# An attention and gated feed-forward kernel: output weights of the second phase moved to the low end of SBUF and sent through DRAM

## The chip, the cores and the metric

The kernel runs on one NeuronCore of a Trainium2 chip. The metric is device time in microseconds (us) of that core. Beside the timed runs, one execution was recorded by the hardware profiler; all durations below come from that execution. The engines are PE (TensorE matmul), PEld (TensorE weight load), DVE (VectorE), ACT (ScalarE), POOL (GpSimd) and SP (SyncE, which in this kernel issues every DMA).

## The reference

The first half is linear attention with exponential features, the second a gated feed-forward layer whose input is the attention's output. Batch 8, heads 8, sequence 576, head size 64, so 4608 tokens of width 512; the feed-forward width is 1536.

```python
def phi(x):
    proj = einsum('bhsd,df->bhsf', x, w_phi)          # 64 -> 128 features
    proj = proj - max(abs(proj), axis=-1, keepdims=True)
    return concatenate([exp(proj), exp(-proj)], axis=-1)
q_p, k_p = phi(q), phi(k)
kv = einsum('bhsf,bhsd->bhfd', k_p, v); z = sum(k_p, axis=2)
attn = einsum('bhsf,bhfd->bhsd', q_p, kv) / (einsum('bhsf,bhf->bhs', q_p, z)[..., None] + 1e-6)

x = attn.transpose(0, 2, 1, 3).reshape(4608, 512)
gate = 1 / (1 + exp(-(x @ w_gate)))                   # 512 -> 1536
out = (gate * (x @ w_val)) @ w_out                    # 1536 -> 512
```

The weights w_gate, w_val and w_out arrive in 64 bits.

## The kernel before, in words

**Precision.** A feed-forward factor is held as two 32-bit parts in TensorE's rounded format (fp32r): a high part and the rest. A product takes three matmuls: high by high, high by rest, rest by high. The function `weigh` loads a 512 KB block of 64-bit weights and makes both parts on DVE and ACT.

**First phase.** The 32 attention steps (8 batches by 4 head pairs, `attend`) run together with the feed-forward layer of the first 4 of the 12 blocks of 128 hidden units. `gate` (matmuls at L913) makes gate and value for a chunk of 512 tokens, `first_js` (matmuls at L970) multiplies by the 4 blocks of output weights; the partial sums go to DRAM (`ys`). After the last attention step only the feed-forward work of the chunks 7 and 8 is left, and with it begins the preparation of what follows.

**Second phase.** The other 8 blocks are taken in 4 pairs n = 0 to 3. Gate and value weights of a pair are combined by `combine` into seven products in place of eight (a Strassen scheme, so a weight tile G has 7 parts); `out_weight` makes the two parts of one block of output weights. Two passes go over all tokens, six stretches of 768 tokens each: the first with the pairs 0 and 1, the second with 2 and 3. One stretch is a call of `pass_over`: 28 products of six matmuls with 384 moving columns (L1228: stationary G, moving X), then 72 matmuls with 512 moving columns (L1310: stationary the gated values h, moving the output weights wo). During the first four stretches of pass one, the weights of the pairs 2 and 3 are made, put into a staging ring, written to DRAM (`kept`), and read back before pass two (`fetched`).

**Where the tiles lie.** Each partition of SBUF holds, from the low end, a few constants, the tile `flat`, and the tile `low`; from the high end down, during the first phase, the attention's tiles, and after it the tiles `more` and `high`. In the built program `low` begins at 50 KB and `high` at 137 KB. Rings of buffers are cut out of these tiles: X, y1, h and the staging ring lie in `low` (h at 48 to 72 KB from its start, staging at 72 to 86), G and the ring of output weights `r_wo` in `high` (G at 0 to 56 KB, `r_wo` at 56 to 72). In the first phase `low` holds that phase's weights (0 to 32), its x (32 to 48), its output weights (48 to 64) and its h (64 to 84); only the x of chunk 7 lies in `high`, at 42 to 58 KB. In a profile row `bank<-low,high` or `gate<-high,low` means that one operand lies in each tile, and `gate<-low` that both lie in `low`.

**What sets the order.** A planner (`Plan.run`) walks through all operations with a rank and an assumed duration each and writes one fixed order for PE, DVE, ACT and SP. A ring slot is given to the operation when the planner reaches it. Two marks hold operations back: `last` opens the `high` and `more` tiles after the last attention step, and `done` stands for the end of the whole first phase.

Of the kernel before, what the change touches and what calls it, by code (L numbers as in the profile page):

```python
# [20 lines left out]
P = 128  # L21
NP = H // 2
DM = H * D
# [12 lines left out]
DC = 2 * HT  # L36
NDC = NT // DC
CELL = 64
RA = 86 << 10
RB = 72 << 10  # L40
FB = 15 << 10
NQ = 3
LATE = 7
# [16 lines left out]
KEEP = 30.0  # L60
# [207 lines left out]
def attention_moe(  # L268
# [21 lines left out]
    def ring(where, tag, n, width, dtype=F32):  # L290
        cells, made = Cells(n), {}

        def view(i):
            if i not in made:
                pool = stage[where] if isinstance(where, str) else where
                made[i] = pool.tile([P, width], dtype, tag=f"{tag}{i}", name=f"{tag}{i}")
            return made[i]

        return [Slot(cells, i, 1, lambda i=i: view(i)) for i in range(n)]

    def arena(where, name, size, dtype):
        made = []

        def view():
            if not made:
                pool = stage[where] if isinstance(where, str) else where
                made.append(pool.tile([P, size // 4], dtype, tag=name, name=name))
            return made[0]

        cells = Cells(size // CELL)  # L310
        return lambda start=0: Area(view, cells, start * 1024 // CELL)
# [19 lines left out]
    wscr = [dram.tile([2, P, DM], F32, tag=f"wo{j}", name=f"wo{j}") for j in range(NJ)]  # L331
# [8 lines left out]
    r_g = ring(ps, "gate", 8 - BANKS, DM)  # L340
    low, high = arena(ff, "low", RA, F32R), arena("two", "high", RB, F32R)
    flat, more = arena(ff, "flat", 32 << 10, F32), arena("two", "more", FB, F32)
    x = low()
# [4 lines left out]
    x = flat()  # L348
# [4 lines left out]
    x = low()  # L353
    r_X = x.ring(14, 2 * HT)
    r_y1 = x.ring(3, DM)
    r_h = x.ring(8, 2 * HT)
    r_stage = x.ring(2, 7 * 2 * P)
    x = high()
    r_G = x.ring(8, 7 * 2 * P)
    r_wo = x.ring(8, DM)  # L360
    r_x7 = high(42).ring(2 * NC4, CW)
    r_sum = flat(20).ring(1, 2 * DM)
    r_tmp = flat(24).ring(1, 2 * HT)
# [1 line left out]
    x = more()  # L365
# [4 lines left out]
    def at(tag, n, shape, dtype=None):  # L370
        width = 1
        for s in shape[1:]:
            width *= s
        if tag not in at_rings:
            at_rings[tag] = ring("at", tag, n, width, dtype or F32)
        return Buf([at_rings[tag]], shape)
# [12 lines left out]
    def sp(size, fn, reads, writes, rank, after=()):  # L389
        return plan.op("SP", 0.06, size, fn, reads, writes, rank, after=after)  # L390
# [7 lines left out]
    def due(i):  # L398
        return 11.0 * i if i < NP else START + PERIOD * (i - NP)
# [7 lines left out]
    def attend(i):  # L407
        b, p = steps[i]
        r, slack = due(i), 0.1 if i < 2 * NP else 0.5
# [119 lines left out]
        else:  # L529
            nj = 2 * S // 32  # L530
# [11 lines left out]
            for hd in range(2):  # L542
                on_act(
                    DM, lambda hd=hd: act.copy(d()[:, hd, :DM], qf[hd]()),  # L544
# [6 lines left out]
                ),  # L551
                [pt], [(d, 2)], r + 2,
            )
            pm, pn = at("pm", 2, [P, nj]), at("pn", 2, [P, nj])
            mb = at("mb", 1, [P, 2, S])
            dve(
                2 * S,
# [445 lines left out]
    for i in range(N):  # L1003
# [8 lines left out]
        if i % NP == NP - 1:  # L1012
            lo = 0 if i < NP else ((i // NP) * S) // CW
            for c in range(lo, ((i // NP + 1) * S) // CW):
# [7 lines left out]
                r = due(i + 1) + LEAD + 66.0 * (c - lo)  # L1022
# [19 lines left out]
    done = plan.op("X", 0.0, 0.0, lambda: None, after=opening)  # L1042
# [7 lines left out]
    def pair(n):  # L1050
        return JA + 2 * n, JA + 2 * n + 1
# [49 lines left out]
    def kept(bufs, where, mark, r):  # L1101

        for n, x in enumerate(bufs):
            sp(
                x.shape[1] << 9,
                lambda n=n, x=x: nc.sync.dma_start(where[n], x().bitcast(F32)),
                [x], [(mark, n)], r,
            )

    def fetched(rings, width, where, mark, r, after=()):  # L1110

        out = []
        for n in range(2):
            x = Buf(rings, [P, width])
            sp(
                width << 9,
                lambda n=n, x=x: nc.sync.dma_start(x().bitcast(F32), where[n]),
                [(mark, n)], [x], r, after,
            )
            out.append(x)  # L1120
        return out

    def out_weight(j, r, rings, after):
        wh, wl = Buf(rings, [P, DM]), Buf(rings, [P, DM])
        weigh(j, 2, r, False, wh, wl, slice(0, DM), None, after)
        return wh, wl
# [166 lines left out]
    def pass_over(ns, dc, r, ws, wo, src, mark, dst, dmark):  # L1293

        x = x_blocks(dc, r - XLEAD)
        hs = []
        for i, n in enumerate(ns):
            hs.append([(Buf([r_h], [P, 2, HT]), Buf([r_h], [P, 2, HT])) for _ in range(2)])
            gs = gated(group(ws[n, 0], x, r + 14.6 * i))
            valued(gs, group(ws[n, 1], x, r + 14.6 * i + 7.3), hs[i])  # L1300
        for T in range(DC // P):
            acc = Buf([r_g], [P, DM])
            h, o = divmod(T * P, HT)
            for i, n in enumerate(ns):

                def out_part(i=i, n=n, acc=acc, h=h, o=o):
                    for e, j in enumerate(pair(n)):
                        (hh, hl), (wh, wl) = hs[i][e], wo[j]
                        for k_, (s, w) in enumerate(((hh, wh), (hh, wl), (hl, wh))):
                            nc.tensor.matmul(  # L1310
                                acc(), s()[:, h, o : o + P], w(),
                                start=i + e + k_ == 0, stop=i + e + k_ == 4,
                            )

                outs.append(pe(
                    "f", 1.37, out_part,
                    [(y, h) for hl_ in hs[i] for y in hl_]
                    + [y for j in pair(n) for y in wo[j]],
                    [acc], r + 29.2 + 1.4 * T + 0.7 * i, 0.3,
                ))  # L1320
            finish(dc * (DC // P) + T, acc, src, mark, dst, dmark, r + 29.2 + 2.8 * T)
# [6 lines left out]
    ws, wo, marks = {}, {}, {}  # L1328
    for n in range(2):
        r = base - 30.0 + 30.0 * n  # L1330
        for m in range(2):
            ws[n, m] = combine(n, m, r + 10.0 * m, [r_G], [])
        for j in pair(n):
            wo[j] = out_weight(j, r + 20.0, [r_wo], [])
    start = base + 150.0
    for dc in range(NDC):
        r = start + SPAN * dc
        pass_over(
            (0, 1), dc, r, ws, wo, yscr, ymark, lambda c, t: y2scr[c][t], y2mark
        )  # L1340
        if dc < 4:
            n, m = 2 + dc // 2, dc % 2
            mark = marks[n, m] = Buf()
            kept(combine(n, m, r + KEEP, [r_stage], [done]), gscr[n, m], mark, r + KEEP)
            j = JA + 4 + dc
            mark = marks[j] = Buf()
            kept(out_weight(j, r + KEEP + 10.0, [r_stage], [done]), wscr[j], mark, r + KEEP)

    start += SPAN * NDC
    for n, m, late in ((2, 0, []), (2, 1, taken[-4:-3]), (3, 0, outs[-8:-7]), (3, 1, outs[-1:])):  # L1350
# [66 lines left out]
```

## Time and profile before

| | |
|---|---|
| median of 3 runs | 1168.27 us (1164.08, 1168.27, 1170.7) |
| the profiled execution | 1167.91 us, of it the span from the first to the last instruction 1166.0 us |
| PE busy | 1148.7 us, 99% of the span, 8796 matmuls |
| DVE, ACT busy | 933.6 us (80%), 583.3 us (50%) |
| DMA | 166.88 MB, 143 GB/s in the mean |
| granted TensorE clock | 1.000 throughout |
| L1228 / L1310 / L913 / L970, matmul | 2016 / 864 / 804 / 432 instructions |

Times in the trace count from the span's start. Attention ends near 516 us, the first phase's last matmul near 613 us; pass one runs from there to 890 us, pass two to the end. A busy PE is not a PE at its peak, since the ends of matmuls are modelled: what one matmul costs in a dense stretch is the stretch's length over the number of its matmuls.

### The profile page before, as it was taken

The numbers are of one execution on the slowest core, as the hardware profiler recorded it, in microseconds if no ns is written. First come the engines' busy times: TensorE is split into PE (matmuls) and PEld (weight loads), VectorE is DVE, ScalarE is ACT, GpSimd is POOL, SyncE is SP. The second block draws the span as 40 slices with busy tenths as digits, with TensorE's granted clock in tenths as the row PEclk, the third lists the DMA queues.
The fourth block names the chain that finished last, engine by engine and source line by source line (L and its number), as shares of the span: only waits on it lengthen the run. The fifth ranks groups of instructions, "written<-read, shape, count | busy, mean of one in ns | idle before, by whom it ended". The sixth has DMA issues, their size and how long they took to land.

```text
span 1166.0 us, 22301 instructions
## 1 busy us (share of the span) xinstructions
PE 1148.7 (99%) x8796; PEld 939.5 (81%) x8796; DVE 933.6 (80%) x1793; ACT 583.3 (50%) x1115; POOL 0.7 (0%) x6
## 2 busy tenths in 40 slices
PE   8999999999999999999999999999999999999998
PEld 6666566776676777778879899899899898998997
DVE  6999989888878878848987999998766756857764
ACT  6767776666657666626553444352332332423421
POOL 0000000000000000000000000000000000000000
PEclk9999999999999999999999999999999999999999
DMA  7674553444425353225334646645557424224232
GB/s 235 202 242 126 151 169 120 133 125 126 146 80 160 108 155 103 79 79 193 116 99 152 204 142 238 181 147 179 163 178 278 143 93 122 81 89 157 59 91 82
DMA packets 97136, 166.88 MB, mean 143 GB/s; under 512 B 18568, under 2 KB 43272, under 8 KB 97032
## 3 DMA queue, kind: packets, MB, share of 16 engines
q1 hardware_dynamic: 97032, 165.46, 44.8%
q8 instruction: 69, 1.13, 0.4%
q14 instruction: 35, 0.29, 0.1%
HBM read 117.96 MB, written 47.32 MB: 142 GB/s over the span
## 4 chain that ended last, share of the span: by engine, by line
PE 85%; DVE 8%; DMA 5%; ACT 1%; issue 1%; SPq 0%; DVEq 0%; ACTq 0%
PE bank L1228 30%; PE gate L1310 17%; PE gate L913 11%; PE gate L970 7%; PE bank L620 4%; PE bank L662 3%; PE bank L431 2%; DMA rb<-den 2%; PE bank L680 2%; PE bank L913 2%; PE bank L536 1%; DMA den<-dn 1%; PE bank L970 1%; DVE d L586 1%; PE bank L634 1%; PE bank L646 1%
## 5 line engine op out<-in xcount | busy, mean ns | idle before, releaser
L1228 PE MATMUL bank<-low,high 128*128 128x384 f32 x2016 | 352.3, 336 | 0.9 <-DVE low L1190 0.7
L1228 PEld LDWEIGHTS bank<-low,high 128*128 128x128 f32 x2016 | 349.8, 188 | 2.7 <-DVE low L1190 1.0
L1310 PE MATMUL gate<-high,low 128*128 128x512 f32 x864 | 203.6, 395 | 0.0
L1310 PEld LDWEIGHTS gate<-high,low 128*128 128x128 f32 x864 | 162.3, 188 | 37.9
L913 PE MATMUL gate<-low 128*128 128x512 f32 x708 | 168.4, 394 | 1.2 <-ACT flat L948 0.6
L913 PEld LDWEIGHTS gate<-low 128*128 128x128 f32 x708 | 130.8, 188 | 30.2 <-issue 1.2
L478 ACT ACTIVATE ek<-ek 128x512 f32<-128x512 f32 (+1 forms) x192 | 96.7, 526 | 27.5 <-DVE ek L466 26.2
L1241 DVE TENSOR_TENSOR more<-more,bank 128x384 f32<-128x384 f32 x104 | 57.2, 550 | 43.0 <-PE bank L1228 42.8
L970 PE MATMUL gate<-low 128*128 128x512 f32 x372 | 89.8, 395 | 0.0
L970 PEld LDWEIGHTS gate<-low 128*128 128x128 f32 x372 | 68.6, 188 | 15.0 <-issue 1.0
L620 PE MATMUL bank<-ek,vin 128*32 128x256 f32 x1240 | 73.3, 381 | 4.5 <-ACT d L544 4.1
L1241 DVE TENSOR_TENSOR flat<-flat,bank 128x384 f32<-128x384 f32 x87 | 47.9, 551 | 34.9 <-PE bank L1228 34.2
L620 PEld LDWEIGHTS bank<-ek,vin 128*32 128x32 f32 x1240 | 37.4, 110 | 45.8 <-issue 10.2
L1138 DVE TENSOR_TENSOR flat<-gate,low 128x512 f32<-128x512 f32 x72 | 49.3, 685 | 24.8 <-PE gate L1310 15.0
L437 DVE TENSOR_REDUCE mk<-bank 128x4 f32<-128x512 f32 (+1 forms) x92 | 49.0, 551 | 19.7 <-PE bank L431 17.1
L1186 ACT CAST low<-more 128x768 fp32r<-128x768 f32 x36 | 30.1, 836 | 66.2 <-DVE more L1177 66.2
L466 DVE TENSOR_TENSOR ek<-bank,mk 128x512 f32<-128x512 f32 (+1 forms) x92 | 48.2, 550 | 0.6 <-ACT d L549 0.2
L937 ACT CAST low<-flat 128x512 fp32r<-128x512 f32 x36 | 22.3, 621 | 49.6 <-DVE flat L962 45.4
L589 ACT ACTIVATE eq<-d 128x1152 f32<-128x1152 f32 x29 | 33.9, 1167 | 24.5 <-DVE d L586 24.4
L1283 ACT CAST low<-flat 128x384 fp32r<-128x384 f32 x44 | 22.0, 511 | 45.0 <-DVE flat L1279 44.9
L1266 ACT ACTIVATE more<-more 128x384 f32<-128x384 f32 x37 | 19.4, 525 | 47.6 <-DVE more L1241 47.6
L431 PE MATMUL bank<-wk,kin 64*128 64x128 f32 x496 | 38.5, 289 | 4.5 <-DMA kin<-k 4.4
(187 smaller groups left out, 1701.0 us busy)
## 6 DMA issues: line engine op xcount, KB each, us to landing
flat<-w_moe SPq DMA_DIRECT2D x36, 512.0 KB
low<-xs SPq DMA_DIRECT2D x46, 256.0 KB
kin<-k SPq DMA_DIRECT2D x32, 320.0 KB
qin<-q SPq DMA_DIRECT2D x32, 320.0 KB
vin<-v SPq DMA_DIRECT2D x32, 320.0 KB
ys<-flat SPq DMA_DIRECT2D x36, 256.0 KB
low<-ys SPq DMA_DIRECT2D x36, 256.0 KB
yt<-flat SPq DMA_DIRECT2D x36, 256.0 KB
```

The lines of the kernel that those rows point to most:

```text
L431: nc.tensor.matmul(pk[hd]()[:, t, :], x()[head(hd), t * P : t * P + P], wk[head(hd), :], start=True, stop=True,)
L437: vec.tensor_reduce(mx, pk, axis=AX.X, op=ALU.max, apply_absolute_value=True)
L466: vec.tensor_tensor(ek[g]()[:, :, F:], src, mk[g]()[:, :ns].unsqueeze(2).broadcast_to([P, ns, F]), op=ALU.subtract,)
L478: lambda g=g, sg=sg: act.activation(ek[g]()[:, :, sg * F : sg * F + F], ek[g]()[:, :, F:], AF.Exp, scale=1.0 - 2.0 * sg,),
L620: nc.tensor.matmul(o_[o : o + Q, : 2 * F], vx()[:, 2 * t + hd, o % D : o % D + Q], (e0, e1)[hd][:, t, :] if t < 4 else e2[:, 0, :], start= ...
L662: nc.tensor.matmul(nm()[o : o + Q, :], w()[:, sg, o : o + Q], es[sg]()[:, o // D, cs], start=sg == 0, stop=sg == 1, tile_position=(0, o),)
L913: nc.tensor.matmul(o(), a()[:, ws], x(), start=cc + n == 0, stop=cc == NC4 - 1 and n == 2,)
L970: nc.tensor.matmul(acc(), a()[:, ts], w(), start=first and i == 0, stop=last and i == 2)
L1138: lambda: vec.tensor_tensor(y(), acc(), y1().bitcast(F32), op=ALU.add),
L1228: nc.tensor.matmul(o()[:, :HT], s()[:, ws], y()[:, cc, :], start=first and cc + i_ == 0, stop=cc + i_ == 3, skip_group_check=not first,)
L1241: lambda: vec.tensor_tensor(o(), p(), q()[:, :HT], op=ALU.add),
L1310: nc.tensor.matmul(acc(), s()[:, h, o : o + P], w(), start=i + e + k_ == 0, stop=i + e + k_ == 4,)
```

## The change

Five things are done.

1. The ring `r_wo` of 8 output-weight buffers (2 KB each) goes from `high` to `low`, where it takes 72 to 88 KB from the tile's start (122 to 138 KB of the partition in the built program), behind h. `low` grows from 86 to 88 KB, `high` shrinks from 72 to 70.
2. The staging ring goes from `low` to `high`, behind G (56 to 70 KB). A second ring `r_swo` of 7 buffers of 2 KB covers the same 14 KB; staged output weights take those instead of the 7 KB buffers.
3. Since `low` is in use until the first phase ends, the output weights of the pairs 0 and 1 can no longer be made in their final place. They are made in `r_swo`, written to DRAM, and read back after `done`: 8 writes and 8 reads of 256 KB more.
4. The attention's small tiles `pm` and `pn` get one buffer each in place of two.
5. Through the planner the order of instructions moves: on SP from about 533 us of the trace on, on DVE, ACT and PE from about 550. Up to there it is the same.

```diff
-RA = 86 << 10
-RB = 72 << 10
+RA = 88 << 10
+RB = 70 << 10
...
     r_h = x.ring(8, 2 * HT)
-    r_stage = x.ring(2, 7 * 2 * P)
+    r_wo = x.ring(8, DM)
     x = high()
     r_G = x.ring(8, 7 * 2 * P)
-    r_wo = x.ring(8, DM)
+    r_stage = x.ring(2, 7 * 2 * P)
+    r_swo = high(56).ring(7, DM)
     r_x7 = high(42).ring(2 * NC4, CW)
...
-            pm, pn = at("pm", 2, [P, nj]), at("pn", 2, [P, nj])
+            pm, pn = at("pm", 1, [P, nj]), at("pn", 1, [P, nj])
...
         for j in pair(n):
-            wo[j] = out_weight(j, r + 20.0, [r_wo], [])
+            mark = marks[j] = Buf()
+            kept(out_weight(j, r + 20.0, [r_swo], []), wscr[j], mark, r + 20.0)
     start = base + 150.0
+    for j in (*pair(0), *pair(1)):
+        wo[j] = fetched([r_wo], DM, wscr[j], marks[j], start - 20.0, [done])
...
             j = JA + 4 + dc
             mark = marks[j] = Buf()
-            kept(out_weight(j, r + KEEP + 10.0, [r_stage], [done]), wscr[j], mark, r + KEEP)
+            kept(out_weight(j, r + KEEP + 10.0, [r_swo], [done]), wscr[j], mark, r + KEEP)
```

In the changed file the lines L913, L970 and L1228 stand at L914, L971 and L1229, L1310 at L1311 and the DMA of `fetched` at L1118.

**PE, where the first phase ends.** L913 are the last gate and value products of chunk 8, L970 its output products (48 matmuls, in four rows of 12), L1228 the first products of the second phase. Before:

```order
L913 MATMUL bank_194<-low 128x512 x12
L1228 MATMUL bank_192<-low,high 128x384 x6
L1228 MATMUL bank_182<-low,high 128x384 x6
L970 MATMUL gate_213<-low 128x512 x12
L970 MATMUL gate_206<-low 128x512 x12
L970 MATMUL gate_219<-low 128x512 x12
L970 MATMUL bank_180<-low 128x512 x12
L1228 MATMUL bank_204<-low,high 128x384 x6
```

After:

```order
L914 MATMUL bank_194<-low 128x512 x12
L1229 MATMUL bank_192<-low,high 128x384 x6
L971 MATMUL gate_213<-low 128x512 x12
L971 MATMUL gate_206<-low 128x512 x12
L971 MATMUL gate_219<-low 128x512 x12
L971 MATMUL bank_182<-low 128x512 x12
L1229 MATMUL bank_180<-low,high 128x384 x6
L1229 MATMUL bank_204<-low,high 128x384 x6
```

The second product of the second phase now stands behind chunk 8's output products. In the same way one value product of chunk 8 now stands ahead of chunk 7's output products, near 569 us of the trace. Beyond these two places PE's order is the same to the end.

**SP, at the same place.** `ys8` are the sums of chunk 8, written from `flat`; `ys0` the partial sums that the first stretch reads; `w_moe` the 64-bit weights of pair 2. Before:

```order
L999 DMA ys8_105<-flat_175 128x512 x2
L1166 DMA more_5903<-xs2_90 128x2x384
L999 DMA ys8_105<-flat_175 128x512 x2
L1133 DMA low_325<-ys0_97 128x512 x3
L790 DMA flat_175<-w_moe 128x1024 x3
L1166 DMA low_325<-xs1_89 128x2x256
```

After:

```order
L1167 DMA more_5848<-xs2_90 128x2x384
L1000 DMA ys8_105<-flat_175 128x512
L1118 DMA low_325<-wo4_119 128x512 x2
L1118 DMA low_325<-wo5_120 128x512 x2
L1118 DMA low_325<-wo6_121 128x512 x2
L1118 DMA low_325<-wo7_122 128x512 x2
L1134 DMA low_325<-ys0_97 128x512 x3
L791 DMA flat_175<-w_moe 128x1024 x2
L1167 DMA low_325<-xs1_89 128x2x256
```

The eight reads of the output weights stand between the last sums of chunk 8 and the reads of `ys0`; of the three weight loads behind them, the third has moved further back.

## The prediction, made before the changed kernel ran

> **What bounds the kernel now.** I read the busy times, PE's waits, and then the chain of waits, in order of time, where it runs along PE.
>
> ```profile
> PE 1148.7 (99%) x8796; PEld 939.5 (81%) x8796; DVE 933.6 (80%) x1793; ACT 583.3 (50%) x1115; POOL 0.7 (0%) x6
> ...
> PE bank L1228 <- DVE low L1190: 0.7, 1, 0.7
> ...
> PE bank L1228 <- ACT low L1186: 0.2, 1, 0.2
> ```
>
> PE is busy for 99% of the span. These two are its only waits after the attention, 0.9 us together, both at 600 us. So no wait is left to take away beyond that place: time after 516 us falls only if a matmul gets cheaper. A busy share does not tell what one costs; pieces of the chain without a gap do, by their length over their count:
>
> ```profile
> 532.93 5.60 PE bank L913 x24
> ...
> 549.43 8.40 PE bank L913 x36
> 557.83 8.40 PE gate L913 x36
> ...
> 568.97 10.88 PE bank L970 x48
> 579.85 8.16 PE gate L913 x36
> ...
> 613.37 27.04 PE bank L1228 x156
> 640.41 16.79 PE gate L1310 x72
> ```
>
> All but L1228 have 512 moving columns. L970 costs 10.88/48 = 226.7 ns, and so does L913 at 579.85 (8.16/36). L1310 costs 16.79/72 = 233.2, and L913 from 532.93 to 566 (5.60/24, 8.40/36) 233.3. Same line, same shape, same clock (1.000), two prices. What differs is where the operands lie (order of time, PE):
>
> ```profile
> 549.27 6.93 PE L913 MATMUL bank<-high,low 128*128 128x512 f32 x29
> ...
> 568.81 11.04 PE L970 MATMUL bank<-low 128*128 128x512 f32 x48
> 579.69 8.32 PE L913 MATMUL gate<-low 128*128 128x512 f32 x36
> ...
> 640.25 5.06 PE L1310 MATMUL gate<-high,low 128*128 128x512 f32 x21
> ```
>
> The dear ones read the moving operand from `high` (x of chunk 7; output weights) and the stationary one from `low`; the cheap ones read both from `low`. L1228 has it the other way round, moving X in `low` and stationary G in `high`, and costs 27.04/156 = 173.3 ns for 384 columns. The step from 384 to 512 columns that this leaves to the low price, 226.7 - 173.3 = 53.4 ns, is exactly 128 columns at 2.4 per ns, so L1228 carries the low price's fixed part (226.7 - 213.3 = 13.4 ns) and not the high price's 19.9. It is the moving operand's place that costs 6.6 ns.
>
> **The change part by part.**
>
> *Output weights to `low`.* The 864 matmuls of L1310 keep their stationary h in `low` and get the moving operand from there too. There are 12 groups of 72, each 16.79 us now and 72 x 226.7 ns = 16.32 us at the low price: 12 x 0.47 = 5.6 us less. Bounds: the trace shows the low price for moving operands up to 64 KB into `low` (114 KB of the partition) and the high price from 42 KB into `high` (179 KB); the new place is at 122 to 138 KB. Unknown lies between, so the gain is between 0 and 5.6. I take 5.6: the new place is 8 KB from the last cheap one and 41 KB from the first dear one; and by distance between the operands too it is near (at most 40 KB from h; the cheap pairs of L913 are up to 48 KB apart, the dear pairs at least 71).
>
> One rule speaks against it. The Trainium skill ("SBUF — State Buffer", Who interferes with whom) gives PE two independent read ports, one for the moving operand and one for weight loads, and says that PE waits on nobody; in "TensorE: Matmul & The Clock Gate" (Back-to-back issue gap) the gap hangs on the column count alone. By that, moving the weights brings 0; the trace's 226.7 against 233.3 ns on one line disagrees, though nothing in it is a test of the place alone. It is a rival below.
>
> *The second product of pass one behind L970.* Around PE's only late wait (order of time, PE, then DVE):
>
> ```profile
> 598.73 1.21 PE L1228 MATMUL bank<-low,high 128*128 128x384 f32 x6
> 600.16 0.44 PE L1228 MATMUL bank<-low,high 128*128 128x384 f32 x1 [0.23 <-ACT low L1186]
> 601.31 1.14 PE L1228 MATMUL bank<-low,high 128*128 128x384 f32 x5 [0.70 <-DVE low L1190]
> 602.29 8.36 PE L970 MATMUL gate<-low 128*128 128x512 f32 x36
> ```
>
> ```profile
> 599.11 0.68 DVE L934 TENSOR_TENSOR flat<-flat,bank 128x512 f32<-128x512 f32 x1
> 599.71 0.68 DVE L866 SCALAR_TENSOR_TENSOR high<-flat 128x512 fp32r<-128x512 uint32 x1
> 600.31 0.95 DVE L1190 TENSOR_TENSOR low<-more,low 128x768 fp32r<-128x768 f32 x1
> 601.18 0.68 DVE L939 TENSOR_TENSOR low<-flat,low 128x512 fp32r<-128x512 f32 x1
> ```
>
> Two products, 6 x 173.3 ns = 1.04 us each, fill 598.73 to 602.29: 3.56 - 2.08 = 1.48 us is lost, waiting for the second product's X (L1186, L1190). Now one product ends at 599.77 and L970 follows. Its first 9 matmuls need only h of blocks made earlier: 9 x 0.227 = 2.04 us, to 601.8. The last three need the last h, whose rest L939 writes until 601.86 here; in the changed order one short DVE operation and one of L1190's size stand between L934 and L939, and on ACT a copy of the first product's sum stands ahead of the cast that L939 needs: much the same in the end. The 12th matmul, the only one that reads it, starts near 602.3. So no wait follows: 1.48 us gained. Bounds: 0 (DVE late by as much) to 1.48. The product that moved finds its X 10.9 us later, long done. The value product of chunk 8 that passes chunk 7's sums only swaps two pieces of work without a wait between 566 and 590 us: nothing.
>
> *The round trip of the output weights.* 8 writes and 8 reads of 256 KB on SP. The price of an issue and the rate come from where pass two's weights are read (order of time, SP; a window of 4 us, whose last column is GB/s; the page's mean and its 40 slices):
>
> ```profile
> 890.28 1.82 SPq L1117 DMA_DIRECT2D high<-wo  x4
> 892.15 0.90 SPq L1117 DMA_DIRECT2D high<-g  x2
> 893.15 2.17 SPq L1117 DMA_DIRECT2D high<-wo  x4
> ...
> 894.00:898.00 4.00, 4.00 (x25) 4.00 (x24) 1.81 (x4) 1.11 (x3) 0.00 (x0) 1.00 1.05 396
> ...
> DMA packets 97136, 166.88 MB, mean 143 GB/s; under 512 B 18568, under 2 KB 43272, under 8 KB 97032
> ...
> GB/s 235 202 242 126 151 169 120 133 125 126 146 80 160 108 155 103 79 79 193 116 99 152 204 142 238 181 147 179 163 178 278 143 93 122 81 89 157 59 91 82
> ```
>
> An issue takes about 0.5 us, and 396 GB/s are reached. The reads stand behind the last sums of chunk 8, which wait for the end of L970:
>
> ```profile
> 611.36 3.04 SPq L999 DMA_DIRECT2D ys<-flat  x2
> 614.49 1.62 SPq L1133 DMA_DIRECT2D low<-ys  x3
> 616.16 16.99 SPq L790 DMA_DIRECT2D flat<-w_moe  x3
> ```
>
> L970 now starts at 599.77 and ends near 610.8 instead of 613.4, so the reads are issued from about 612 to 616; 2.1 MB take 5 us at that rate and 15 at the mean of 143 GB/s. L1310 first needs them at 640.41 - 1.48 = 638.9: 8 us spare at the worst. What waits behind them on SP moves by 4 us: `ys0`, first read when L1310 has its first sums, and the weights of pair 2 (order of time, DVE):
>
> ```profile
> 624.30 0.42 DVE L795 TENSOR_SCALAR flat<-flat 128x512 uint32<-128x512 uint32 x1
> ```
>
> DVE takes the first of these up at 624.30 without a wait, 8 us after its issue; in the changed order that operation stands 11 DVE operations later, near 629. Cover suffices for 4 us of issue and 5 of transfer. The price if it doesn't: every us that DVE stands still there goes to PE as soon as the 5 banks are full. The writes come while the chunks 7 and 8 are worked off, and each waits in SP's queue for ACT or DVE to finish a part; behind them wait weight loads for pairs 0 and 1, which nobody needs before 598.73. I take 0, and 2 us as the upper bound.
>
> *Staging in `high`.* ACT and DVE write the same parts with the same instructions at another address; between 640 and 800 us, where DVE is fullest, it has room (after the length: busy us and count of PE, PEld, DVE, ACT, POOL):
>
> ```profile
> 640.00:680.00 40.00, 40.00 (x208) 36.74 (x207) 37.25 (x70) 17.96 (x34) 0.00 (x0) 1.00 0.61 204
> 680.00:720.00 40.00, 40.00 (x208) 36.74 (x207) 39.44 (x75) 17.41 (x33) 0.00 (x0) 1.00 0.59 198
> 720.00:760.00 40.00, 40.00 (x208) 36.74 (x207) 37.56 (x69) 17.61 (x32) 0.00 (x0) 1.00 0.56 165
> 760.00:800.00 40.00, 40.00 (x207) 36.74 (x206) 37.83 (x69) 15.14 (x27) 0.00 (x0) 1.00 0.58 190
> ```
>
> 152.1 us in 160, while PE gets through with the same work 3.5 x 0.47 = 1.6 us sooner: 6 us remain. Taken as 0; the second of these windows alone has 0.6 us to spare, so 0 to 2.
>
> *One buffer for `pm` and `pn`.* Both are written and read by DVE alone, in order: 0.
>
> *The sum*, against the profiled execution: 1167.9 - 5.6 - 1.5 = 1160.8 us. The median of the runs is 0.4 above the profiled one: **1161.1 us**, 0.61% below 1168.27.
>
> **The rivals.**
>
> *A. The price changes inside the new place*, at 128 KB of the partition, say. Three of the eight buffers lie below that, and by the built program 324 of the 864 matmuls read them: 324 x 6.6 ns = 2.1 us in place of 5.6, so 1164.6. For it: the 65 KB between cheap and dear are unseen in the trace. Against: the place is at the cheap end of them. 15%.
>
> *B. The place has nothing to do with it*, and the high price belongs to something else that chunk 7 and L1310 share. Only the 1.5 us of PE's wait go: 1166.8. The skill's two pages named above give this one. Against: L913 changes price at 566 within one line. 10%.
>
> *C. DVE becomes the limit after the phase change*, on the late weights of pair 2 or in the window from 680 to 720: 2 to 4 us come back, about 1164. For it: DVE's 39.44 of 40. Against: PE waits for DVE nowhere there now. 13%.
>
> *D. The output weights come late* (the other side). The first group of L1310 waits for all eight reads; from 638.9 on each us late is a us lost, and from 646 on the gain of 7.1 is eaten. For 1174 and more they must land after 652, 2.1 MB in 40 us, under 55 GB/s. One slice of the page is that low (59), but of little demand. 5%, and 1177 if so.
>
> **How the numbers follow.** The forecast keeps 57%. About 0.5% (5.8 us) is what a measurement of this kernel tells from no change; the limit for faster is 1162.4, 1.3 us above the forecast, and the three runs before lie 6.6 us apart, so I count 0.8 of the forecast as faster by over 0.5% (0.46), with a little from A and C (0.04): 0.50. Slower by over 0.5%: D, 0.05. Within 0.5%: 0.45. The range goes from 1159 (the forecast less the runs' scatter) to 1167 (B included).
>
> **What would show it.** Right: L1311 in pieces of 72 at 16.3 us, its names `gate<-low`; L914 on `high,low` still 233 ns; no wait of PE at 600 us; L971's last group ending about 2.5 us sooner; the reads of the output weights on SP from 612 on, none waited for. Wrong: L1311 at 233 ns throughout (B) or a mix of the two prices (A); PE waiting for DVE between 625 and 800 (C), or for a DMA at 639 (D).

## The result, and the profile after

The changed kernel takes 1160.76 us (median of 8 runs, 1159.15 to 1161.92), the kernel before 1167.71 us (8 runs, 1164.08 to 1170.7). The ratio is 0.9935, with a 95% interval of 0.9923 to 0.9948: 0.65% less. The profiled execution has a span of 1158.9 us, 7.1 us less than the 1166.0 before.

The chain of waits of the changed kernel, in order of time (start, length, what), around the end of the first phase and at the end of the program:

```profile
489.49 10.89 PE gate L971 x48
...
549.04 8.40 PE bank L914 x36
...
598.50 1.04 PE bank L1229 x6
599.54 8.20 PE gate L971 x36
607.74 2.72 PE bank L971 x12
610.46 28.08 PE bank L1229 x162
638.54 16.36 PE gate L1311 x72
654.90 29.12 PE bank L1229 x168
...
1138.86 16.37 PE gate L1311 x72
```

Two things are to be seen. From 598.50 to 654.90 each piece begins where the one before it ends: PE's wait at 600 us is gone, and no other has come. And a group of 72 output products, whose rows now read `gate<-low`, takes 16.36 us where it took 16.79. Chunk 7's products at 549 us, whose x still lies in `high`, cost 8.40 us for 36 as before. The last group of the kernel before, and the start of the same L970 group, give the length of the stretch that the change can touch:

```profile
489.81 10.94 PE gate L970 x48
...
1145.53 16.81 PE gate L1310 x72
```

From the start of that group to the start of the first output products it was 640.41 - 489.81 = 150.60 us and is 149.05, so 1.55 less; from there to the end of the last group it was 521.93 us and is 516.69, so 5.24 less. Together 6.79 of the 7.1 us; the other 0.3 lie before 490 us, where the profiles of the kernels below differ by more than that.

The output weights are read back without anyone waiting for them (SP in the changed kernel, order of time):

```profile
611.54 4.12 SPq L1118 DMA_DIRECT2D low<-wo  x8
...
617.95 1.87 SPq L791 DMA_DIRECT2D flat<-w_moe  x2
```

DVE is fuller than before in its fullest window (after the length: busy us and count of PE, PEld, DVE, ACT, POOL), 39.86 of 40 us where it was 39.44, and PE has no idle time in it:

```profile
680.00:720.00 40.00, 40.00 (x211) 37.16 (x210) 39.86 (x76) 17.59 (x33) 0.00 (x0) 1.00 0.59 198
```

### The profile page after: what moved, and what is told of

It reads as the page before. It is cut to its first block, busy times and chain, and to the rows that moved or that the text cites. A ratio compares the mean times of both kernels' runs of the same rounds, so it can differ in the third digit from the quotient of the medians.

```text
span 1158.9 us, 22323 instructions
## 1 busy us (share of the span) xinstructions
PE 1142.8 (99%) x8796; PEld 939.5 (81%) x8796; DVE 933.3 (81%) x1793; ACT 583.0 (50%) x1115; POOL 0.7 (0%) x6
## 4 chain that ended last, share of the span: by engine, by line
PE 84%; DVE 7%; DMA 6%; ACT 2%; issue 1%; SPq 1%; DVEq 0%
PE bank L1229 30%; PE gate L1311 17%; PE gate L914 11%; PE gate L971 6%; PE bank L621 4%; PE bank L663 3%; PE bank L914 3%; DMA rb<-den 3%; PE bank L432 2%; PE bank L681 2%; DMA den<-dn 2%; PE bank L537 1%; DVE d L587 1%; PE bank L971 1%; PE bank L635 1%; PE bank L647 1%
## 5 line engine op out<-in xcount | busy, mean ns | idle before, releaser
L1229 PE MATMUL bank<-low,high 128*128 128x384 f32 x2016 | 351.8, 336 | 0.0
L1229 PEld LDWEIGHTS bank<-low,high 128*128 128x128 f32 x2016 | 349.8, 188 | 1.1
L1311 PE MATMUL gate<-low 128*128 128x512 f32 x864 | 198.4, 389 | 0.0
L1311 PEld LDWEIGHTS gate<-low 128*128 128x128 f32 x864 | 162.0, 188 | 33.2
L914 PE MATMUL gate<-low 128*128 128x512 f32 x696 | 165.7, 393 | 1.2 <-ACT flat L949 0.6
L914 PEld LDWEIGHTS gate<-low 128*128 128x128 f32 x696 | 128.6, 188 | 29.7 <-issue 1.2
L1242 DVE TENSOR_TENSOR more<-more,bank 128x384 f32<-128x384 f32 x111 | 61.1, 551 | 40.8 <-PE bank L1229 40.3
L971 PE MATMUL gate<-low 128*128 128x512 f32 x384 | 92.3, 394 | 0.0
L971 PEld LDWEIGHTS gate<-low 128*128 128x128 f32 x384 | 70.8, 188 | 15.1 <-issue 1.0
L1242 DVE TENSOR_TENSOR flat<-flat,bank 128x384 f32<-128x384 f32 x75 | 41.3, 551 | 29.3 <-PE bank L1229 29.1
L1284 ACT CAST low<-more 128x384 fp32r<-128x384 f32 x50 | 24.7, 513 | 46.6 <-DVE more L1280 46.6
L590 ACT ACTIVATE eq<-d 128x1152 f32<-128x1152 f32 x29 | 33.9, 1168 | 24.8 <-DVE d L587 24.4
```

Source lines behind the costliest of these rows:

```text
L914: nc.tensor.matmul(o(), a()[:, ws], x(), start=cc + n == 0, stop=cc == NC4 - 1 and n == 2,)
L971: nc.tensor.matmul(acc(), a()[:, ts], w(), start=first and i == 0, stop=last and i == 2)
L1229: nc.tensor.matmul(o()[:, :HT], s()[:, ws], y()[:, cc, :], start=first and cc + i_ == 0, stop=cc + i_ == 3, skip_group_check=not first,)
L1242: lambda: vec.tensor_tensor(o(), p(), q()[:, :HT], op=ALU.add),
L1311: nc.tensor.matmul(acc(), s()[:, h, o : o + P], w(), start=i + e + k_ == 0, stop=i + e + k_ == 4,)
```

## The experiments

Each changed kernel moves the whole time by a few us, and single runs of one kernel lie up to 8 us apart. Most of that scatter arises in the first 250 us: the same L913 piece of the attention starts at 249.98 us in the profile of the kernel before, at 247.28 and 252.43 in two of the kernels below, and from there to the L970 group at 490 us all three take 239.84 us within 0.02. So each kernel is read twice, by its median and by the two stretches named above, from its profile. Each ratio is to runs of the kernel before that were taken together with the kernel's own. One table for all:

| kernel | median, us | ratio to before | to the first output products | from there to the end |
|---|---|---|---|---|
| before | 1167.71 to 1168.93 in four sets of runs | | 150.60 | 521.93 |
| the change | 1160.76 | 0.9935 (0.9923 to 0.9948) | 149.05 | 516.69 |
| e2: round trip and order, old place | 1168.42 | 0.9993 (0.998 to 1.0005) | 149.12 | 523.52 |
| e3: order alone | 1166.16 | 0.9979 (0.997 to 0.9987) | 150.10 | 521.93 |
| e4: change, old order | 1165.80 | 0.998 (0.9966 to 0.9993) | 155.18 | 516.87 |
| e6: before, `high` 64 bytes lower | 1174.54 | 1.0051 (1.0037 to 1.0066) | 150.96 | 526.71 |
| e7: change, `high` 64 bytes lower | 1166.90 | 0.9979 (0.9966 to 0.9991) | 149.47 | 521.85 |
| e8: before, `low` 64 bytes higher | 1172.53 | 1.0038 (1.0026 to 1.005) | 150.94 | 526.57 |
| e9: before, `high` 192 bytes lower | 1165.36 | 0.9973 (0.996 to 0.9985) | 150.35 | 517.10 |
| e10: change, `high` 192 bytes lower | 1161.50 | 0.9942 (0.9929 to 0.9955) | 148.42 | 517.02 |
| e11: change, h behind the output weights and 64 bytes higher | 1165.95 | 0.9983 (0.9972 to 0.9994) | 149.05 | 522.56 |

### The place by itself (e1)

```diff
+    for st in "afkpuy":            # stationary tile at 16, 56, 96, 136, 176, 208 KB
+        for mv in NAMES:           # moving tile a..y, every 8 KB
+            for i in range(36):
+                nc.tensor.matmul(o, tiles[st][:, s : s + P], tiles[mv][:, m : m + DM], ...)
```

> A measurement by itself: the whole computation of the reference is left out and the output holds ones. 25 tiles of 8 KB lie side by side in SBUF, from 16 KB of the partition to 216 KB. For each of six stationary tiles (at 16, 56, 96, 136, 176 and 208 KB) every tile in turn is the moving operand of 36 matmuls of 128x512 in fp32r. Theory P (the moving operand's own address decides): 226.7 ns for every moving tile up to some address between 138 and 179 KB, 233.3 ns above it, with the same step for all six stationary tiles. Theory Q (the distance between the two operands decides): 226.7 ns while they lie at most 48 KB apart, 233.3 ns from 71 KB on, so that the cheap stretch travels with the stationary tile and both ends of the row are dear when it lies in the middle. Theory R (the place has no part in it, rival B of the prediction): the same price for all 150 pairs.

PE in this kernel, order of time, the first blocks after the start (moving tile, stationary tile):

```profile
12.82 8.32 PE L38 MATMUL acc<-tb,ta 128*128 128x512 f32 x36
20.98 8.32 PE L38 MATMUL acc<-tc,ta 128*128 128x512 f32 x36
```

From start to start 8.16 us for 36, that is 226.7 ns. All 149 blocks behind the first have this length, wherever their operands lie. Theory R holds, P and Q fall: neither the region of SBUF nor the distance across regions costs anything, as long as the operands lie whole multiples of 512 bytes apart, as all of these do. The prediction's reading, that "the moving operand's place" costs 6.6 ns, falls with them, while the time that it forecast had come out. So the price hung on something that the place carried along.

### The change taken apart (e2, e3, e4)

e2 is the kernel before with the round trip, but into the old buffers; e3 only holds the second product back; e4 is the change with that product forced ahead again:

```diff
 # e2, on the kernel before
-            wo[j] = out_weight(j, r + 20.0, [r_wo], [])
+            mark = marks[j] = Buf()
+            kept(out_weight(j, r + 20.0, [r_wo], []), wscr[j], mark, r + 20.0)
     start = base + 150.0
+    for j in (*pair(0), *pair(1)):
+        wo[j] = fetched([r_wo], DM, wscr[j], marks[j], start - 20.0, [done])
 # e3, on the kernel before (product of pass_over)
+            late = [done] if i and len(taken) < 2 else []
-            o_ = pe("f", 1.05, go, [gh, gl, xh, xl], [o], r + 1.04 * i, 0.3, taken[-1:])
+            o_ = pe("f", 1.05, go, [gh, gl, xh, xl], [o], r + 1.04 * i, 0.3, taken[-1:] + late)
 # e4, on the change (closers: the output products of chunk 8)
+            if i == 1 and len(taken) == 1:
+                for cl in closers:
+                    o_.then.append(cl)
+                    cl.wait += 1
```

> The kernel before with the output weights of the first pairs written to DRAM and read back as in the change, but into their old buffers in `high`: the round trip and the order of PE that it brings, without the new place. Theory (the place gives 5.2 of the 7 us, the order 1.5): the groups of 72 of the output product stay at 16.79 us, PE's wait at 600 us is gone, about 1166.2 us by the median, 1.5 below the kernel before. Rival B (the place has nothing to do with it): about 1161, as the change. If the round trip itself cost something that the change hides: over 1168.

> The kernel before, in which the second product of the first pass may not start before the last output product of chunk 8 is planned: the order alone, with no round trip, and no new place. Theory: groups of 72 at 16.79 us, no wait of PE at 600 us, 1.5 us below the kernel before, about 1166.2 us. Rival (the wait only goes elsewhere, to the last of chunk 8's output products, whose operand DVE writes last): a PE wait of 1 to 1.5 us between 600 and 612 us, and the time of the kernel before, 1167.7.

> The changed kernel with the second product of the first pass put back ahead of chunk 8's last output products, as the kernel before had it: new place and round trip, without the order. Theory: groups of 72 at 16.36 us as in the change, PE's wait of about 1.5 us at 600 us back, about 1162.3 us, 1.5 above the change and 5.4 below the kernel before. Rival (the order is the larger part of the gain): over 1165.

The output groups behave as expected in all three. The chains of e2, e3 and e4, one piece each:

```profile
636.24 16.79 PE gate L1310 x72
```

```profile
640.42 16.79 PE gate L1311 x72
```

```profile
643.49 16.36 PE gate L1318 x72
```

The totals don't follow the theories: forecast were 1166.2, 1166.2 and 1162.3 us, measured 1168.42, 1166.16 and 1165.80, and the one that met its number did not do so for the reason given. Every edit lets the planner write another order elsewhere, and each new order brought a stall of its own.

**e2** wins the first stretch, 149.12 us, 1.48 less than before: the order alone is worth the 1.48 us that were forecast. It loses 1.59 in the second, around the third output group, whose sums come late; PE's wait is 1.0 of it, and the matmuls around the wait run less densely:

```profile
PE gate L1310 <- DVE flat L1138: 1.0, 1, 1.0
```

So its median, 1168.42, is that of the kernel before. In this order, the round trip without a new price of the matmuls brings nothing.

**e3** shows what the prediction feared as rival C. Its chain leaves PE for a weight read (in order of time):

```profile
600.44 8.18 PE gate L970 x36
...
614.42 6.21 DMA flat<-w_moe
623.09 7.64 PE bank L1228 x42
630.76 9.66 PE bank L1228 x54
```

and on DVE the first operation on those weights stands still for them:

```profile
620.66 0.43 DVE L795 TENSOR_SCALAR flat<-flat 128x512 uint32<-128x512 uint32 x1 [2.47 <-DMA flat<-w_moe]
```

Of the 2.47 us, 1.0 reaches PE: the first stretch is 0.50 us shorter, not 1.5. In the change the same reads are issued 3.5 us later (617.95 against 614.42), but DVE's order has its operation later still, and it does not wait. The median of e3 is 2.1 us below that of before, of which its profile explains the 0.5; where the rest comes from is open.

**e4** keeps the output groups at 16.36 and loses 6.13 us in the first stretch, not 1.5. PE's waits and the granted clock tell why (windows: after the length, busy us and count of PE, PEld, DVE, ACT, POOL, then the granted clock):

```profile
PE bank L1232 <- ACT low L1190: 2.1, 1, 2.1
...
PE bank L1232 <- DVE low L1194: 0.7, 1, 0.7
```

```profile
596.00:600.00 4.00, 2.36 (x12) 1.82 (x10) 4.00 (x8) 2.41 (x5) 0.00 (x0) 1.00 0.00 0
600.00:602.00 2.00, 0.84 (x2) 0.50 (x3) 2.00 (x4) 0.43 (x1) 0.00 (x0) 0.67 0.00 0
602.00:604.00 2.00, 2.00 (x7) 1.90 (x7) 1.75 (x4) 0.83 (x1) 0.00 (x0) 0.50 0.00 0
604.00:606.00 2.00, 2.00 (x6) 1.53 (x5) 2.00 (x5) 0.00 (x0) 0.00 (x0) 0.50 0.00 0
606.00:608.00 2.00, 2.00 (x7) 1.61 (x6) 1.86 (x3) 0.00 (x0) 0.00 (x0) 0.62 0.00 0
```

After a wait of 2.1 us, and 0.7 us more one matmul later, PE's clock is at half until 607.5 us. The loss of 6.13 us adds up: 2.8 of waiting, 1.5 for the second product's six matmuls, which take 2.50 us in place of 1.04, and 1.9 for the 36 matmuls of L972, which take 10.07 in place of 8.20. The median lies where the rival (the order is the larger part) had it, over 1165, but for another reason. The kernel before waits 0.9 us at this place in two bits and keeps its clock. The length of a wait alone does not decide this, as another place shows, near 142 us in the attention (the kernel before, then the change with its clock):

```profile
144.91 2.37 PE L620 MATMUL bank<-ek,vin 128*32 128x256 f32 x40 [2.64 <-ACT d L544]
```

```profile
142.75 3.61 PE L621 MATMUL bank<-ek,vin 128*32 128x256 f32 x40 [2.39 <-ACT d L545]
...
144.00:146.00 2.00, 2.00 (x24) 1.06 (x20) 1.89 (x7) 1.77 (x5) 0.00 (x0) 0.50 0.24 45
```

The kernel before waits 2.64 us there and keeps the full clock; the change waits 2.39 and is at half for 3.4 us. What decides beside the length was not measured. So the estimate of "1.5 us back" was too low, since it took the wait to be as long as before and left the clock out.

A part of this change can't be taken alone, since the planner's order moves with it. The kernels below (e6 to e11) therefore keep every engine's order word for word and move addresses only.

### By how many bytes the operands are apart (e5)

What else do `low` and `high` differ in? In the built program `low` begins at byte 51232 of the partition and `high` at 140256. Within 128 bytes that is 32 and 96; their difference, 89024, is 347 x 256 + 192. All tiles of e1 lay a multiple of 512 bytes apart.

```diff
+    def series(mv, more, stat, n):
+        for k in range(8):                       # moving operand 16 k bytes further
+            for i in range(36):
+                m, s = (i % 3) * DM + 4 * k + more // 4, (i % 4) * P + stat // 4
+                nc.tensor.matmul(acc[k][:, :n], t["st"][:, s : s + P], t[mv][:, m : m + n], ...)
+    series("near", 0, 0, 512); series("far", 0, 0, 512); series("near", 128, 0, 512)
+    series("far", 4, 0, 512); series("near", 0, 32, 512); series("far", 0, 64, 512)
+    series("near", 0, 96, 512); series("far", 0, 0, 384); series("near", 0, 96, 384); ...
```

> A measurement by itself: the whole computation of the reference is left out and the output holds ones. Each block is 36 matmuls in fp32r with 128 partitions on both sides; the output's name tells by how many bytes the moving operand's address stands above a multiple of 128 (0 to 112 in steps of 16). Series in order: near tile (16 KB of the partition), stationary 0, 512 columns; far tile (188 KB); near, all 128 bytes higher; far, all 4 bytes higher; near with the stationary operand 32 bytes up; far with it 64 up; near with it 96 up; then 384 columns far and near, and 256 columns. All tiles of the first measurement lay at multiples of 128. Theory S (the moving operand's address within 128 bytes decides; `low` lies 32 above a multiple of 128, `high` 96): 226.7 ns at 0 and 32, 233.3 ns at 96, the same near and far and for each place of the stationary operand; 384 columns 173.3 and 180. Theory T (the place never mattered for PE alone, and other engines' or the queues' traffic at `high` slows its reads): 226.7 ns in every block.

Measured, from the starts of the single matmuls (mean of the last 24 of the 35 gaps in a block, ns); columns are the moving operand's address within 128 bytes:

```
                       0     16     32     48     64     80     96    112
near, stationary 0   233.7  231.7  233.3  233.3  228.9  231.1  233.3  231.1
far,  stationary 0   226.7  231.7  233.3  233.3  228.9  231.1  233.3  231.1
far,  stationary 64  233.3  234.6  233.3  226.7  226.7  231.7  233.3  233.3
near, stationary 96  234.4  231.1  233.3  234.6  233.3  226.7  226.7  231.7
```

(The first block stands in the kernel's first microseconds and is not settled.) From column to column the output's bank in PSUM changes too, but it can't be the cause, since the row shifts with the stationary operand. Near and far are alike. But theory S falls: with the stationary operand at 0, 32 is as dear as 96. Theory T falls too: DVE ends at 4 us and the transfers, but for one of 16 KB about every 30 us, at 29 us, while the far row begins at 72 us; and the near blocks beside those transfers cost what the far ones cost. The row moves with the stationary operand: the run 226.7, 231.7, 233.3, 233.3 begins at 0, at 64, at 96, wherever the stationary operand lies. What decides is the difference of the two addresses: theory U. With 256 columns (far, stationary 0) the row is another: 120.0 ns at 0, 113.3 at 112, and 116.7 to 120.0 between.

### 64 bytes in the kernel (e6, e7, e8)

The expectations of these three were written before e5's result was known, so they hold S against T.

```diff
 # e6 on the kernel before, e7 on the change: `high` and `more` start 64 bytes lower
-FB = 15 << 10
+FB = (15 << 10) + 64
 # e8 on the kernel before: `flat` and `low` start 64 bytes higher (lines one lower)
+    const.tile([P, 16], F32, name="pad")
```

> The kernel before with `high` and `more` 64 bytes lower in SBUF, and nothing else: same instructions in the same order on every engine, output weights still in `high`, now 32 bytes above a multiple of 128 where it was 96. Theory S: groups of 72 of the output product 16.36 us (were 16.79), chunk 7's matmuls 226.7 ns (were 233.3), 5.2 + 0.6 us less, 1162.4 us, with PE's wait at 600 us as before. Theory T, or the region as such (64 bytes of 137 KB change no region): 16.79 us and 1168.2 us.

> The changed kernel with `high` and `more` 64 bytes lower, and nothing else. Only chunk 7's x is still read from `high` as the moving operand, 96 matmuls. Theory S: these at 226.7 ns in place of 233.3, 0.6 us less than the change, about 1160.1 us. Theory T: as the change, 1160.8 us.

> The kernel before with 64 unused bytes ahead of `flat` and `low`, so that `low` lies 96 bytes above a multiple of 128, as `high` does; same instructions in the same order. Theory S: every matmul with a moving operand in `low` gets dear: 768 of L914, 432 of L971 and 2016 of L1229 (one line lower than in the kernel before), 6.6 ns each, 21 us more, about 1189 us; L1229's pieces of 168 at 30.2 us (were 29.13). Theory T: no change, 1168.2 us.

S and T miss in all three. Each became dearer than the kernel that it came from, and at a line that no theory had named in e6 and e7. The chains of e6, e7 and e8:

```profile
642.44 16.73 PE gate L1310 x72
659.17 29.57 PE bank L1228 x168
688.74 16.80 PE gate L1310 x72
```

```profile
637.59 16.37 PE gate L1311 x72
653.96 29.58 PE bank L1229 x168
```

```profile
643.15 16.73 PE gate L1311 x72
659.88 29.55 PE bank L1229 x168
```

The gate products cost 29.57/168 = 176.0 ns where they cost 173.4; the 1848 of them in the second stretch make 4.8 us, and it is longer by 4.8 in e6, 5.2 in e7 and 4.6 in e8. U, which came after these expectations, says why: all three take the difference between `low` and `high` to 128 modulo 256 for whatever reads across (the moving X in `low` less the stationary G in `high` was 64), and 384 columns cost 176.0 ns there by the measurement below. Moving one tile up or the other down is the same to it, as measured.

### The decisive bytes (e9, e10, e11)

If U holds, the gain of the change can be had without it, by 192 bytes, and can be taken from it again, by 64.

```diff
 # e9 on the kernel before, e10 on the change
-FB = 15 << 10
+FB = (15 << 10) + 192
 # e11 on the change
-RA = 88 << 10
+RA = (88 << 10) + 64
-    r_h = x.ring(8, 2 * HT)
     r_wo = x.ring(8, DM)
+    x.next += 1
+    r_h = x.ring(8, 2 * HT)
```

> The kernel before with `high` and `more` 192 bytes lower and nothing else; same instructions, same order, output weights in `high`. Theory U (the difference of the two operands' addresses, moving less stationary, modulo 256 bytes decides; by the residue measurement 226.7 ns at 0, 233.3 at 192, 384 columns 173.3 at 0 and 64): this edit takes the output product and chunk 7 from 192 to 0 and the gate product from 64 to 0. Groups of 72 at 16.36 us (were 16.79), chunk 7's 36 matmuls 8.16 us (were 8.40), the gate product's 168 still 29.13 us, PE's wait at 600 us as before: 5.2 + 0.6 us less than the kernel before, about 1162.7 us. If it is the region: no change, 1168.5.

> The changed kernel with `high` and `more` 192 bytes lower and nothing else: every product of the two phases then has its operands a multiple of 256 bytes apart. Theory U: as the change, and chunk 7's 96 matmuls at 226.7 ns, 0.6 us less, about 1160.2 us, the fastest of all. If it is the region: as the change, 1160.8.

> The changed kernel, with output weights and h in `low` in swapped order and 64 unused bytes between them, so that moving less stationary of the output product is 192 modulo 256 again, as in the kernel before; same instructions in the same order, round trip and staging as in the change. Theory U: groups of 72 at 16.79 us, all 5.2 us of the place given back, about 1166.0 us. If it is the region: as the change, 1160.8.

The chains of e9, e10 and e11, in this order:

```profile
582.03 8.16 PE gate L913 x36
...
642.62 16.36 PE gate L1310 x72
658.98 29.14 PE bank L1228 x168
```

```profile
547.75 8.16 PE bank L914 x36
...
636.81 16.36 PE gate L1311 x72
653.17 29.15 PE bank L1229 x168
```

```profile
637.91 16.93 PE gate L1312 x72
...
684.54 16.79 PE gate L1312 x72
701.33 29.12 PE bank L1230 x168
```

Where the operands of these output groups lie (e9, then e11):

```profile
642.46 16.52 PE L1310 MATMUL gate<-high,low 128*128 128x512 f32 x72
```

```profile
684.37 16.95 PE L1312 MATMUL gate<-low 128*128 128x512 f32 x72
```

e9 has the output weights still in `high`, made in place, no round trip, every instruction in its old order, and its output groups cost 16.36 us, as in the change. Its second stretch is 4.83 us shorter than before, its first 0.25: 5.1 of the 5.8 forecast. e11 has the weights in `low` with the change's order, and its groups cost 16.79 again (the first 16.93); its second stretch is 5.87 us longer than the change's, 5.2 by the price and 0.7 in and behind the first group, where the chain of waits passes over DVE. Its median lies where U put it (1165.95, forecast 1166.0). e10 makes chunk 7's products cheap too (8.16 for 36, 226.7 ns, were 8.40): its first stretch is 0.63 us shorter than the change's. A gate product costs a trace more there (29.15 against 29.12 us for 168), so 0.33 goes back, and its median, 1161.5 where 1160.2 was forecast, can't be told from the change's. None of these kernels was shown to take less time than the change.

In one point e9 stays open: its median is 2.65 us below that of before, not 5.8. From 490 us on its profile has 5.1 us less; the L970 group there begins at 492.27 instead of 489.81 us, 2.5 later, though the edit touches nothing that runs before 516 us. A part of it is seen: in e9's profile PE waits 3.26 us near 142 us and is then at half clock for 3.4 us, where the kernel before keeps its clock. In the eleven profiles this group starts at 489.49 to 492.27 us in the five with such a stretch and at 487.12 to 489.81 in the six without. Among the runs with a granted clock of 1.000 the medians are 1163.05 (4 of e9) and 1167.26 (10 of before), 4.2 apart. What the rest is was not shown.

### The period (e12)

> A measurement by itself: the whole computation of the reference is left out and the output holds ones. Blocks of 36 matmuls; first moving less stationary address from 0 to 240 in steps of 16 bytes, with 512 and with 384 columns, three moving and four stationary operands in turn as in the residue measurement; then one fixed pair, 0 to 1984 bytes apart in steps of 64, with 512 and 384 columns. Theory U with period 256: the first 16 blocks repeat the residue measurement (226.7 at 0, 233.3 at 192), and in the fixed pair's series every fourth block has the same price. If the period is longer (512 or 1024), the fixed pair shows it; if the price came from alternating operands, the fixed pair costs 226.7 ns in all blocks.

One fixed pair of operands, 0, 64, 128, 192 and again 256, 320 ... bytes apart (the names count 16 for 64). PE in order of time, 512 columns:

```profile
239.41 8.35 PE L39 MATMUL zero<-near,st 128*128 128x512 f32 x36
247.59 8.42 PE L39 MATMUL sixteen<-near,st 128*128 128x512 f32 x36
255.85 8.53 PE L39 MATMUL thirtytwo<-near,st 128*128 128x512 f32 x36
264.21 8.57 PE L39 MATMUL fortyeight<-near,st 128*128 128x512 f32 x36
272.62 8.37 PE L39 MATMUL sixtyfour<-near,st 128*128 128x512 f32 x36
280.83 8.42 PE L39 MATMUL eighty<-near,st 128*128 128x512 f32 x36
```

The first four lengths repeat from the fifth on, within 0.02 us, through all 32 blocks: the period is 256 bytes. The settled gaps, in ns:

```
difference modulo 256      0      64     128    192
512 columns, fixed pair  226.7  228.9  232.1  233.3
384 columns, fixed pair  173.3  173.3  176.0  174.7
```

The kernels' prices are these: 226.7 for L970 and the change's L1311 (0), 233.3 for the old L1310 (192), 173.4 for the gate products at 64 and at 0, 176.0 at 128. In steps of 16 bytes, three moving and four stationary operands in turn, the differences 0 to 240 cost with 512 columns 226.7 (0 and 240), 228.9 to 231.7 (16, 64, 80, 112) and 232.1 to 234.6 (all others); with 384 columns 173.3 to 176.7, and 180.0 at 240. Repeats agree within 0.1 ns, but for three differences: with 512 columns 240 cost 233.3 in one series of e5 and 226.7 in four others of e5 and e12, and 176 cost 231.1 and 233.3; with 384 columns 160 cost 173.3 and 176.7.

What inside PE collides is not settled. The period and the dependence on both addresses would fit the two reads of a matmul, its moving stream and the weight load of the next one, meeting in the same part of SBUF. No run left one of the two out.

## Why the prediction was right, and where it was not

The forecast was 1161.1 us in a range of 1159 to 1167; 1160.76 came out. The size was right, and the reason given for the larger term was not; that the larger term came out all the same was luck.

- **Output weights at the low price, -5.6 us.** Measured -5.24 in that stretch. What was over-sized: a group of 72 costs 16.36, not 72 x 226.7 ns = 16.32 us, since the first gaps of each group swing between 225 and 240 ns before they settle; 12 x 0.43 = 5.2.
- **"It is the moving operand's place that costs 6.6 ns."** This step failed. Two prices on one line at one clock were read rightly, and so was that they go with where the operands lie. But the trace had only two relations between operand addresses among the feed-forward's 512-column matmuls, 0 and 192 bytes modulo 256, and these coincided with the two tiles. e1 shows all regions alike, e9 makes the old place cheap by 192 bytes, e11 makes the new place dear by 64. The argument from nearness (8 KB from the last cheap place, 41 from the first dear one) carried no weight; the forecast held since h and the output weights now share one tile whose rings lie whole multiples of 256 bytes apart. The step that L1228 "carries the low price's fixed part" was right as a number and wrong as proof: a difference of 64 costs 384 columns nothing, while it would cost 512 columns 2.2 ns.
- **Rival A** (a price that changes inside the new place) did not occur: all 12 groups cost 16.36 to 16.37 us. **Rival B** (the place has nothing to do with it) was right in its first half and wrong in its time: the dear price did belong to something else that chunk 7 and L1310 shared, but the change took that along. It had 10%, and no step of the prediction asked what that could be.
- The Trainium skill ("SBUF — State Buffer", Who interferes with whom) has PE's two read ports independent. By that the price could not depend on the relation of the two addresses. With no other engine at work e12 shows 226.7 to 233.3 ns by that relation only, so this consequence does not hold here; whether it is the ports that collide is open.
- **Second product behind L970, -1.48 us.** Measured -1.55 in the change and -1.48 in e2. That DVE would be in time, "near 602.3", held.
- **Round trip and staging, 0.** Held: no wait for `wo`, and DVE, at 39.86 of 40 us, does not hold up PE. e3 shows how near the edge it was: with DVE's operation on the weights of pair 2 a little earlier in its order, rival C costs 1.0 us.
- **Rival D** (late output weights): the reads were issued from 611.54 to 615.66 us, as forecast, and PE reached the products at 638.54 without a wait.

## What to carry to other kernels

Two prices for one matmul at one clock are a reason to look at the addresses of both operands, not only at the tiles that they lie in: here moving less stationary address modulo 256 bytes decided, and a multiple of 256 was the best for 512 fp32r columns. The best difference goes with the column count: with 384 columns 64 was as good, and with 256 columns 0 was among the dearest (120.0 ns, 113.3 at 112). Pad tiles so that operands that meet keep such a difference, and test a "better place" by a shift of some bytes before paying for a move: 192 bytes of padding took the output products to the same price as the move and the round trip. Where a planner writes the order, an experiment that changes the code moves stalls about; shifts of addresses with the order held word for word gave the cleaner answers.

## What was not expected of the hardware

- The price of a matmul depends on the difference of its operands' addresses modulo 256 bytes: 226.7 to 234.6 ns for 512 columns, 173.3 to 180.0 for 384, in steps of 16 bytes. Four bytes off that grid (e5, far, all moving addresses 4 higher) 512 columns cost 235.5 to 240.0 ns.
- 64 bytes of shift of one tile made a 1168 us kernel 0.5% slower (e6): its gate products, which read across the two tiles, went from 173.4 to 176.0 ns.
- In a long dense stretch a wait of 2.1 us, with 0.7 more right behind it, was followed by a granted clock of 0.50 for 6.8 us (e4), which cost 1.9 us in the 36 matmuls behind alone; 0.9 us in two bits was not (the kernel before). Near 142 us waits of 2.39 (the change) and 3.26 us (e9) were followed by 3.4 us of it, and one of 2.64 (the kernel before) was not, so the length alone does not decide. The Trainium skill ("TensorE: Matmul & The Clock Gate", HAM oscillation — how this bites in real kernels) gives gaps over about 3.4 us as the ones to avoid; here shorter ones sufficed.
